# A reordered opening: batch 0's values loaded ahead of pairs 2 and 3, and the first MLP block begun with two pairs

## The chip, the cores and the metric

The kernel runs on one core of one Trainium2 chip. The metric is the device time of one execution in microseconds (us). Three runs of the kernel before gave 321.23, 321.58 and 321.67 us, a median of 321.58. Shorter is better.

## The reference

The input is q, k and v, each of 8 batches, 8 heads, 576 positions and 64 elements per head, and two matrices w_in (512 x 2048) and w_out (2048 x 512), all in float32. It is attention with a causal window of 64 keys, followed by a two-layer network with a hard-swish between:

```python
scores = scale * np.matmul(q, k.transpose(0, 1, 3, 2))
mask = (rel >= 0) & (rel < 64)            # rel = query position - key position
attn = softmax(np.where(mask, scores, -1e9))
x = np.matmul(attn, v)                    # to (8 * 576) tokens x 512
h = x @ w_in
g = h * np.clip(h + 3.0, 0.0, 6.0) / 6.0
out = g @ w_out                           # 4608 x 512
```

## The kernel before, in words

**Units of work.** The attention is done in pairs of heads: pair t is heads 2g and 2g + 1 of batch b, with t = 4b + g, so pairs 0 to 3 are batch 0 and pairs 4 to 7 are batch 1. The network is done in 9 blocks of 512 tokens (`kb`). Block 0 needs all four pairs of batch 0, since a token's 512 inputs are the outputs of 8 heads. For one block the *first product* gives 16 column blocks (`fc`), each the sum of four matmuls over groups g = 0 to 3, group g being the output of pair g (L485). ScalarE (ACT) and VectorE (DVE) then form hard-swish in `gT` (`hidden`, L497 and L498). The *second product* (L521) takes four token groups, each the sum over the 16 column blocks, and its results go out by L527 and L529.

**Batch 0** has a path of its own, the `_early` functions, once for each pair:

- `load_early_qk` (L108) loads a pair's queries and keys, two DMAs of 144 KB, and `load_early_v` (L127) all of the batch's values, four DMAs of 128 KB and one of 64 KB.
- `t_k` and `t_q` transpose them on TensorE (PE, L214) and copy them to `KT` (DVE, L232) and `QT` (ACT, L223). `t_q` also makes `QZ`, zero-padded copies of the last 64 queries, on DVE (L227).
- `s_early` forms the scores (L244 adds the mask by a product, L252 the scores, L257 those of the last keys from `QZ`), and ACT takes their exponentials (L259, L263).
- `shift_early` (L151, L153) makes a second arrangement of the values, shifted by 64 positions, chunk by chunk: chunk 0 on GpSimd (POOL), chunks 1 to 4 on DVE.
- `pv_early` (L352) multiplies weights with values, and DVE divides by the sums (L361, L362). Pairs 0 and 2 use a buffer of two banks, pairs 1 and 3 two separate banks.
- `x_early` transposes the result (L373), and ACT writes it to `xT` (L376), the input of the first product.

Batches from 1 on use `turn` (L274), `turned` (L281), `s_first`, `s_rest` (L308), `weights`, `pv` (L402), `pv_out` and `x_turned` or `x_`.

**What sets the order.** The schedule is written by hand: each engine runs its instructions in the order of the program text, and a wait holds up all that stands behind it on that engine. All loads go by POOL's one DMA queue, in the order in which POOL issues them, between POOL's other instructions. The order there is: pair 0, the identity's select (L669), pair 1, two selects for the mask (L190), pairs 2 and 3, the values, two parts of w_in of 512 KB (columns 0 to 511 and 512 to 1023, that is column blocks 0 to 3 and 4 to 7), POOL's two copies for chunk 0 (L151, L153), the third part of w_in of 1 MB, six selects for later masks (L197), the first half of w_out (L170), pairs 4 and 5 (L119), the second half of w_out, pairs 6 and 7, and batch 1's values (L138).

**PSUM.** There are eight banks: `ps_o` (one buffer of two banks), `ps_t` (three), `ps_h` (two) and `ps_acc` (one). A tile holds its bank until its last reader is done.

**PE's order in the opening.** 16 warm-up products on zeros (`warm`), transposes of pairs 0 and 1, scores of 0, transposes of 2, scores of 1, transposes of 3, scores of 2, scores of 3, four warm-up products, outputs of pairs 0 and 1, two warm-up products, `x_early(0)`, output of pair 2; then block 0's first product: group 0 of column blocks 0, 1 and 2, `x_early(1)`, output of pair 3, `x_early(2)`, group 1 of blocks 0 to 2, groups 0 and 1 of blocks 3 and 4 in the buffer of two banks (`pair_bank`), `x_early(3)`, group 2 of blocks 0 to 4, and group 3 of these (`complete`). Blocks 5 to 15 follow with all four groups at once. Then two units of the second product, the transposes of pair 4, two more units, and in a loop (L795 on) pairs 5 to 7 with units of the second product between them.

Of the kernel before, what the change touches and what calls it, by code (L numbers as in the profile page):

```python
# [10 lines left out]
F32 = mybir.dt.float32  # L11
# [3 lines left out]
MULT = mybir.AluOpType.mult  # L15
# [9 lines left out]
P = 128  # L25
D = 64
W = 64
# [9 lines left out]
def kernel(  # L37
# [61 lines left out]
    def load_early_qk(pairs, first=0):  # L99
        if first:  # L100
            tiles = staged[0]
        else:
            both = stage.tile([SP, 2, H, R * D], BF16, name="qk6", tag="qk")
            tiles = [both[:, 0], both[:, 1]]
        h = 2 * first
        for n in pairs:
            for t, src in zip(tiles, (q, k)):
                nc.gpsimd.dma_start(  # L108
                    out=t[:, h : h + 2 * n, :],
                    in_=src[0, h : h + 2 * n].rearrange("h (p r) d -> p h (r d)", r=R),  # L110
                )
# [12 lines left out]
    def load_early_v():  # L124
        for m in range(NM):
            n = min(P, S - m * P)
            nc.gpsimd.dma_start(  # L127
                out=Vn[0][:n, m, :, 0:D], in_=v[0, :, m * P : m * P + n, :].rearrange("h s d -> s h d"),
            )
# [28 lines left out]
        nc.sync.dma_start(out=us[0 : P - 32], in_=un[32:P])  # L158
        nc.sync.dma_start(out=us[P - 32 : P, 0], in_=un[0:32, 1])

    def load_w_in(i):
        n = FF // 4
        c = (slice(0, n), slice(n, 2 * n), slice(2 * n, FF))[i]
        nc.gpsimd.dma_start(
            out=win16[:, :, c], in_=moe_w_in[:, c].rearrange("(g p) f -> p g f", p=P)
        )

    def load_w_out(c):
        n = NFC // 2
        nc.gpsimd.dma_start(  # L170
            out=wout16[:, c * n : (c + 1) * n, :],
            in_=moe_w_out[c * n * P : (c + 1) * n * P, :].rearrange("(c p) j -> p c j", p=P),
        )
# [28 lines left out]
    def late_windows():  # L202

        for part in halves:
            select(band, part, -1, 1, -1, 0.0)
            select(band, part, W, -1, 1, 0.0)
            select(first, part, 0, -1, 1, 0.0)

    def transposed_heads(pool, src, g):

        tp = pool.tile([P, R, SP], BF16, name="tp", tag="bk")
        for r in range(R):
            for h in range(2):
                nc.tensor.transpose(  # L214
                    out=tp[h * D : (h + 1) * D, r, :],
                    in_=src[:, 2 * g + h, r * D : (r + 1) * D], identity=ident[:SP, :SP],
                )
        return tp

    def t_q(t):  # L220
        b, g = divmod(t, NG)
        tp = transposed_heads(ps_h, staged[b][0], g)
        nc.scalar.copy(  # L223
            out=QT[t][:].rearrange("q (p r) -> q p r", r=R), in_=tp[:].rearrange("q r p -> q p r"),
        )
        for h in range(2):
            nc.vector.tensor_copy(out=QZ[t][halves[h], h], in_=QT[t][halves[h], S - W : S])  # L227

    def t_k(t):
        b, g = divmod(t, NG)  # L230
        tp = transposed_heads(ps_acc, staged[b][1], g)
        nc.vector.tensor_copy(  # L232
            out=KT[t % 4][:, W:].rearrange("q (p r) -> q p r", r=R),
            in_=tp[:].rearrange("q r p -> q p r"),
        )
# [101 lines left out]
    def pv_early(t):  # L337
        b, g = divmod(t, NG)
        vn, vs, pz, pl = Vn[b % 2], Vs[b % 2], Pz[t % 4], Pl[t % 4]
        if t in (1, 3):  # L340
            os = [ps_h.tile([P, 1, 512], F32, name="oh", tag="bk") for _ in range(2)]
        else:
            os = [ps_o.tile([P, 2, 512], F32, name="o", tag="o")]
        n = len(os)
        for h in range(2):
            hh = 2 * g + h
            o = os[h % n][:, h // n]
            for m in range(NM):
                om = o[:, m * (D + 1) : (m + 1) * (D + 1)]
                for a in range(2):  # L350
                    last = m == NM - 1
                    nc.tensor.matmul(  # L352
                        om[a * W : (a + 1) * W], lhsT=pl[:, h, a * W : (a + 1) * W] if last else pz[:, h, m, a, :],
                        rhs=(vn if a and not last else vs)[:, m, hh, 0 : D + 1], start=True, stop=True,
                    )
        opg = work.tile([P, NM, 2, D], BF16, name="opg")
        for i, o in enumerate(os):
            hs = slice(i, i + 2 // n)
            ov = o[:, :, 0 : NM * (D + 1)].rearrange("p h (m c) -> p h m c", c=D + 1)
            rec = recs[:, t, hs, 0:NM]  # L360
            nc.vector.reciprocal(out=rec.unsqueeze(3), in_=ov[:, :, :, D : D + 1])  # L361
            nc.vector.tensor_tensor(  # L362
                out=opg[:, :, hs].rearrange("p m h d -> p h m d"), in0=ov[:, :, :, 0:D],
                in1=rec.unsqueeze(3).to_broadcast([P, 2 // n, NM, D]), op=MULT,
            )
        opgs[t] = opg

    def x_early(t):
# [98 lines left out]
    def first_units(kb):  # L467
        t0 = kb * TB % XR
        gT = gpool.tile([P, NFC, TB], BF16, name="gT")
        gTs[kb] = gT  # L470

        def unit(fc, gs=range(NG), pool=None, to=None, act=True):
            if fc in halfway:
                hT = halfway.pop(fc)
            elif to is not None:
                hT = to
            else:
                if pool is None:
                    if late[0] == 0:
                        pool = ps_acc if fc == 8 else ps_h if fc in (5, 6, 11, 12) else ps_t  # L480
                    else:
                        pool = ps_t if late[0] == 1 or fc % 2 else ps_h
                hT = pool.tile([P, TB], F32, name="hT", tag="bk")[:]
            for g in gs:
                nc.tensor.matmul(  # L485
                    hT, lhsT=win16[:, g, fc * P : (fc + 1) * P], rhs=xT[:, g, t0 : t0 + TB],
                    start=(g == 0), stop=(g == NG - 1),
                )
# [12 lines left out]

        units[kb] = unit, hidden
        return [lambda fc=fc: unit(fc) for fc in range(NFC)]

# [167 lines left out]
    )  # L672
    load_early_qk((1,), 1)
    window()
    load_early_qk((1,) * (NG - 2), 2)
    for t in KT:
        nc.vector.memset(t[:, 0:W], 0.0)
    for t in QZ:
# [3 lines left out]
    nc.vector.memset(first[:], 1.0)  # L682
    pads(1, nc.vector.memset)
    load_early_v()
    nc.vector.memset(Vs[0][0:W, 0], 0.0)
    for i in range(2):
        load_w_in(i)
    shift_early(0, nc.gpsimd.tensor_copy)
    load_w_in(2)
    late_windows()  # L690
    load_w_out(0)
    staged[1] = load_qk(1, 2)
    load_w_out(1)
    load_qk(1, 2, 2)
    load_v(1, True)
    nc.vector.memset(recs[:], 1.0)
    nc.vector.memset(Pl[0][:], 1.0)
    for t in Pl[1:]:
# [4 lines left out]

    warm(ps_h, 12)
    warm(ps_h, 4, W)
    t_k(0)
    t_q(0)
    t_k(1)
    t_q(1)
    s_early(0)  # L710
    t_k(2)
    t_q(2)
    s_early(1)
    t_k(3)
    t_q(3)
    s_early(2)
    for m in range(1, NM):
        shift_early(m, nc.vector.tensor_copy)
    s_early(3)
    warm(ps_acc, 4)  # L720
    pv_early(0)
    pv_early(1)
    warm(ps_acc, 2)
    x_early(0)
    pv_early(2)
    queue_block(0, 0)
    u = units[0][0]

    def inputs(gs, fcs, **to):
        for fc in fcs:  # L730
            u(fc, gs, **to)

    u(0, (0,), ps_acc)
    inputs((0,), (1, 2), pool=ps_t)
    x_early(1)
    pv_early(3)
    x_early(2)
    inputs((1,), range(3))
    for fc, to in zip((3, 4), pair_bank()):
        u(fc, (0, 1), to=to)  # L740
    x_early(3)
    inputs((2,), range(5))
    complete(0, range(5), (3, 4))
    def group(t, n):

        if t >= 2 * NG:
# [146 lines left out]
```

## Time and profile before

| what | value |
|---|---|
| median of three runs | 321.58 us |
| the profiled execution's own time | 321.83 us |
| its span in the trace | 320.0 us |
| PE busy | 302.5 us, 95% |
| DVE, ACT, POOL busy | 181.1, 184.3 and 124.1 us |
| PE busy from 4 to 14 us | 8.64 of 10 us |
| PE busy from 14 to 20 us | 4.87 of 6 us |
| PE busy from 20 to 40 us | 19.26 of 20 us |
| first product of block 0 begins (L485) | 20.30 us |
| last waiting-free stretch of that product | 26.50 to 36.00 us, 44 matmuls |
| granted clock of PE, mean | 0.996 |

The span is what the trace covers; 1.83 us of the execution's time lie outside it. Times in the trace are counted from the start of the span. "PE busy" counts the time in which at least one matmul was in the array, so that a busy PE isn't always at its peak rate; the products of 128x512 follow each other each 0.216 us in the stretch of 44. The first 40 us are read by the chain of waits, which says what each step was released by, by POOL's timeline, and by the DMA queue in windows.

### The profile page before, as it was taken

The page shows a single profiled execution, that of the slowest core. Times are in us where ns is not written, and L with a number is a line of the kernel's source. Part 1 is how long each engine was busy: PE and PEld are TensorE (multiplying, and loading weights), DVE is VectorE, ACT ScalarE, POOL GpSimd, SP SyncE. Part 2 cuts the span into 40 slices and gives each one's busy share as a digit, 9 for nine tenths or more (in the row PEclk, how much of TensorE's full clock was granted, in tenths as well). Part 3 has the DMA queues.
Part 4 walks back from the last instruction along what each step waited for, and adds up shares of the span by engine and source line. Part 5 has one row for each costly group of instructions (what it writes and reads, how often), then busy time and mean ns, then how long its engine had stood idle before and what let it go on. Part 6 is the DMA issues. An engine that isn't in the chain of part 4 may idle for free.

```text
span 320.0 us, 10694 instructions
## 1 busy us (share of the span) xinstructions
PE 302.5 (95%) x4566; PEld 152.2 (48%) x4608; DVE 181.1 (57%) x415; ACT 184.3 (58%) x345; POOL 124.1 (39%) x169
## 2 busy tenths in 40 slices
PE   7889998889999999999999999999999999999992
PEld 3454454444545555555555555555544444444440
DVE  5776747588747753775377627762776156334200
ACT  2737665578657764776477547764773366454310
POOL 8971204669785435553446335633330000000000
PEclk9999999999999999999999999999999999999998
DMA  7999995989999932994299339934021200100021
GB/s 93 164 203 207 207 189 116 173 146 111 179 124 167 131 116 88 167 128 117 88 155 140 108 98 154 144 102 103 5 63 43 84 33 0 69 33 34 36 74 66
DMA packets 57592, 35.67 MB, mean 111 GB/s; under 512 B 39872, under 2 KB 51648, under 8 KB 57536
## 3 DMA queue, kind: packets, MB, share of 16 engines
q0 software_dynamic: 35904, 18.81, 45.9%
q1 hardware_dynamic: 21632, 16.08, 20.6%
q8 instruction: 38, 0.62, 0.8%
q14 instruction: 18, 0.15, 0.1%
HBM read 37.62 MB, written 9.44 MB: 147 GB/s over the span
## 4 chain that ended last, share of the span: by engine, by line
PE 86%; DMA 5%; DVE 2%; issue 2%; ACT 2%; POOL 1%; SPq 0%; POOLq 0%; ACTq 0%
PE hT L485 37%; PE acc L521 35%; PE o L402 3%; PE s L308 3%; PE acco L521 2%; DMA V<-V 2%; PE tk L274 2%; DMA qk<-in_k_dram 2%; DMA xT<-opl 1%; POOL qk L108 1%; PE tq L274 1%; PE hTo L485 1%; DVE opl L426 0%; DVE V L151 0%; PE xp L373 0%
## 5 line engine op out<-in xcount | busy, mean ns | idle before, releaser
L498 DVE SCALAR_TENSOR_TENSOR gT<-t,hT 128x512 bf16<-128x512 bf16 x141 | 95.7, 686 | 77.7 <-ACT t L497 76.9
L485 PE MATMUL hT<-xT,win 128*128 128x512 bf16 x552 | 132.1, 379 | 0.9 <-ACT xT L376 0.3
L521 PE MATMUL acc<-wout,gT 128*128 128x512 bf16 x518 | 126.1, 379 | 2.4 <-issue 1.3
L497 ACT ACTIVATE t<-hT,half_const 128x512 bf16<-128x512 f32 x141 | 95.7, 689 | 50.0 <-PE hT L485 48.1
L485 PEld LDWEIGHTS <-win 128*128 128x128 bf16 x576 | 55.6, 98 | 66.2 <-issue 1.0
L521 PEld LDWEIGHTS <-gT 128*128 128x128 bf16 x576 | 54.3, 98 | 62.8
L329 POOL TENSOR_TENSOR Pz<-e,band 128x512 bf16<-128x512 bf16 x48 | 54.2, 1146 | 0.5 <-ACT e L321 0.4
L326 POOL TENSOR_TENSOR P<-e,first 64x256 bf16<-64x256 bf16 x24 | 15.9, 661 | 84.7 <-ACT e L317 84.6
L527 ACT COPY osb<-acc 128x512 f32<-128x512 f32 x34 | 19.9, 586 | 43.7 <-PE acc L521 43.7
L321 ACT ACTIVATE e<-s 128x512 bf16<-128x512 f32 x56 | 30.2, 593 | 0.9 <-PE s L308 0.7
L281 DVE COPY KT<-tk 128x576 bf16<-128x576 bf16 x28 | 21.0, 749 | 5.3 <-ACT e L317 4.5
L138 POOL DMA_DIRECT2D V<-in_v_dram x22 | 17.9, 819 | 11.6 <-DMA win<-in_moe_w_in_dram 5.2
L426 DVE TENSOR_TENSOR opl<-o,recs 128x256 bf16<-128x256 f32 x52 | 19.6, 419 | 0.5
L281 ACT COPY QT<-tq 128x576 bf16<-128x576 bf16 x28 | 17.8, 637 | 1.5 <-PE tq L274 1.5
L411 DVE TENSOR_REDUCE sums<-o 128x10 f32<-128x20 f32 x26 | 4.5, 175 | 24.3 <-PE o L402 24.3
L402 PEld LDWEIGHTS <-Pz 64*64 64x64 bf16 x1008 | 11.6, 108 | 13.3 <-issue 11.5
L308 PE MATMUL s<-QT,KT 64*64 64x64 bf16 x896 | 14.7, 195 | 0.5 <-issue 0.5
L317 ACT ACTIVATE e<-tk 64x128 bf16<-64x128 f32 x28 | 7.6, 270 | 12.5 <-PE tq L294 12.5
L402 PE MATMUL o<-V,Pz 64*64 64x65 bf16 x936 | 13.6, 195 | 1.2 <-DMA V<-V 1.2
L274 PE MATMUL tk<-ident,qk 64*64 64x64 bf16 x504 | 13.9, 195 | 0.3 <-DMA qk<-in_k_dram 0.3
L274 PE MATMUL tq<-ident,qk 64*64 64x64 bf16 x504 | 13.7, 195 | 0.4 <-DMA qk<-in_q_dram 0.4
L274 PEld LDWEIGHTS <-qk 64*64 64x64 bf16 x1008 | 11.5, 106 | 3.1 <-issue 1.7
(102 smaller groups left out, 196.6 us busy)
## 6 DMA issues: line engine op xcount, KB each, us to landing
out_dram<-osb SPq DMA_DIRECT2D x36, 256.0 KB, 2.3
V<-in_v_dram POOLq DMA_DIRECT2D x16, 256.0 KB, 5.7
V<-V SPq DMA_DIRECT2D x6, 432.0 KB, 4.3
qk<-in_k_dram POOLq DMA_DIRECT2D x4, 576.0 KB, 6.7
qk<-in_q_dram POOLq DMA_DIRECT2D x4, 576.0 KB, 9.7
wout<-in_moe_w_out_dram POOLq DMA_DIRECT2D x2, 1024.0 KB, 18.8
qk<-in_q_dram POOLq DMA_DIRECT2D x12, 144.0 KB, 4.3
qk<-in_k_dram POOLq DMA_DIRECT2D x12, 144.0 KB, 3.8
```

The costliest lines, as they stand in the source:

```text
L274: nc.tensor.transpose(out=hosts[t][z][halves[h], r * W : (r + 1) * W], in_=staged[b][halves[z], 2 * g + h, r * D : (r + 1) * D], identity= ...
L281: (nc.scalar.copy if z else nc.vector.tensor_copy)(out=(QT[t % 4][:] if z else KT[t % 4][:, W:]).rearrange("q (p r) -> q p r", r=RL), in_= ...
L308: nc.tensor.matmul(ss[h][halves[i], c, m, r], lhsT=keys(t, h, W * (w - 1), r), rhs=QT[t % 4][halves[h], w * W : (w + 1) * W], start=True, ...
L321: nc.scalar.activation(out=e[:].rearrange("p c m r w -> p (c m r w)"), in_=ss[h][:].rearrange("p c m r w -> p (c m r w)"), func=EXP, scale ...
L329: muls[h].tensor_tensor(out=Pw[t % 4][:, h].rearrange("p c m r w -> p (c m) (r w)"), in0=e[:].rearrange("p c m r w -> p (c m) (r w)"), in1 ...
L402: nc.tensor.matmul(o[i][halves[c], c0 : c0 + D + 1], lhsT=p, rhs=vt[:, hh, v0 : v0 + D + 1], start=(r == 0), stop=(r == 1), skip_group_che ...
L426: nc.vector.tensor_tensor(out=opg[:, :, i], in0=ov[i][:, 0:4, 1 : D + 1].rearrange("p (m h) d -> p m h d", h=2), in1=rec[:, i, 0:4].rearra ...
L485: nc.tensor.matmul(hT, lhsT=win16[:, g, fc * P : (fc + 1) * P], rhs=xT[:, g, t0 : t0 + TB], start=(g == 0), stop=(g == NG - 1),)
L497: nc.scalar.activation(out=t1[:], in_=hT, func=RELU, bias=half_const[:], scale=1.0 / 6.0)
L498: nc.vector.scalar_tensor_tensor(out=gT[:, fc, :], in0=t1[:], scalar=1.0, in1=hT, op0=MIN, op1=MULT)
L521: nc.tensor.matmul(acc, lhsT=gT[:, fc, ts * P : (ts + 1) * P], rhs=wout16[:, fc, :], start=(fc == 0), stop=(fc == NFC - 1),)
L527: nc.scalar.copy(out=osb[:], in_=acc)
```

## The change

- The loads of pairs 2 and 3 move behind the values. Pair 2's come right after them, then POOL's two shift copies, then pair 3's.
- The first part of w_in is loaded in two halves (groups 0 and 1, then 2 and 3), so there are four issues instead of three; all stand behind pair 3's.
- `QZ` is made by a function of its own, `padded`, on DVE for pairs 0 and 1 and on POOL for pairs 2 and 3. POOL's later issues (six selects, w_out, batch 1) come behind that of pair 3 in the program.
- PE's order: transposes of 0 and 1, scores of 0 and 1, four warm-up products, output of 0, transposes of 2, `x_early(0)`, output of 1, scores of 2, transposes of 3, `x_early(1)`, group 0 of column block 0, output of 2, scores of 3, group 0 of blocks 1 and 2, group 1 of blocks 0 to 2, `x_early(2)`, output of 3, groups 0 and 1 of blocks 3 and 4, group 2 of blocks 0 to 2, `x_early(3)`, group 2 of blocks 3 and 4, and group 3 of the five. Two warm-up products are left out.
- DVE's seven shift copies stand ahead of all of pairs 2 and 3's work.
- All pairs' outputs use the buffer of two banks, chunk by chunk with both heads in turn, with one reciprocal and one product on DVE. Column blocks 0 and 1 stand in `ps_h`, 2 in `ps_acc`, 3 and 4 in `ps_t`. Pair 3's transposes swap their pools.

```diff
-    def load_w_in(i):
+    def load_w_in(i, gs=slice(0, NG)):
...
-            out=win16[:, :, c], in_=moe_w_in[:, c].rearrange("(g p) f -> p g f", p=P)
+            out=win16[:, gs, c], in_=moe_w_in[gs.start * P : gs.stop * P, c].rearrange("(g p) f -> p g f", p=P)
...
-        for h in range(2):
-            nc.vector.tensor_copy(out=QZ[t][halves[h], h], in_=QT[t][halves[h], S - W : S])
+
+    def padded(t, move):
+        for h in range(2):
+            move(out=QZ[t][halves[h], h], in_=QT[t][halves[h], S - W : S])
...
-        if t in (1, 3):
-            os = [ps_h.tile([P, 1, 512], F32, name="oh", tag="bk") for _ in range(2)]
-        else:
-            os = [ps_o.tile([P, 2, 512], F32, name="o", tag="o")]
...
+        o = ps_o.tile([P, 2, 512], F32, name="o", tag="o")
+        for m in range(NM):
+            for h in range(2):
...
-                    if late[0] == 0:
-                        pool = ps_acc if fc == 8 else ps_h if fc in (5, 6, 11, 12) else ps_t
+                        pool = ps_acc if fc == 8 else ps_h if fc in (6, 7, 11, 12) else ps_t
...
     load_early_qk((1,), 1)
     window()
-    load_early_qk((1,) * (NG - 2), 2)
...
     load_early_v()
+    load_early_qk((1,), 2)
     nc.vector.memset(Vs[0][0:W, 0], 0.0)
-    for i in range(2):
-        load_w_in(i)
     shift_early(0, nc.gpsimd.tensor_copy)
-    load_w_in(2)
+    load_early_qk((1,), 3)
+    for gs, c in ((0, 0), (1, 0)):
+        load_w_in(c, slice(2 * gs, 2 * gs + 2))
+    for c in (1, 2):
+        load_w_in(c)
...
+    dve, pool = nc.vector.tensor_copy, nc.gpsimd.tensor_copy
+    for t in range(2):
+        t_k(t)
+        t_q(t)
+        padded(t, dve)
+    s_early(0)
+    s_early(1)
+    for m in range(1, NM):
+        shift_early(m, dve)
+    warm(ps_acc, 4)
+    pv_early(0)
+    t_k(2)
+    t_q(2)
+    padded(2, pool)
+    x_early(0)
+    pv_early(1)
+    s_early(2)
+    t_k(3)
+    t_q(3)
+    padded(3, pool)
     late_windows()
     load_w_out(0)
...
+    x_early(1)
     queue_block(0, 0)
...
+    inputs((0,), (0,), pool=ps_h)
+    pv_early(2)
+    s_early(3)
+    inputs((0,), (1,), pool=ps_h)
+    inputs((0,), (2,), pool=ps_acc)
+    inputs((1,), range(3))
+    x_early(2)
     pv_early(3)
-    x_early(2)
-    inputs((1,), range(3))
-    for fc, to in zip((3, 4), pair_bank()):
-        u(fc, (0, 1), to=to)
+    inputs((0, 1), (3, 4), pool=ps_t)
+    inputs((2,), range(3))
     x_early(3)
-    inputs((2,), range(5))
-    complete(0, range(5), (3, 4))
+    inputs((2,), (3, 4))
+    complete(0, range(5))
```

More of the change, by code (lines that the diff above doesn't have):

```diff
@@ L221, in t_q @@
         b, g = divmod(t, NG)
-        tp = transposed_heads(ps_h, staged[b][0], g)
+        tp = transposed_heads(ps_acc if t == NG - 1 else ps_h, staged[b][0], g)
         nc.scalar.copy(
@@ L225, in t_q @@
         )
+    def padded(t, move):
         for h in range(2):
-            nc.vector.tensor_copy(out=QZ[t][halves[h], h], in_=QT[t][halves[h], S - W : S])
+            move(out=QZ[t][halves[h], h], in_=QT[t][halves[h], S - W : S])
     def t_k(t):
         b, g = divmod(t, NG)
-        tp = transposed_heads(ps_acc, staged[b][1], g)
+        tp = transposed_heads(ps_h if t == NG - 1 else ps_acc, staged[b][1], g)
         nc.vector.tensor_copy(
@@ L339, in pv_early @@
         vn, vs, pz, pl = Vn[b % 2], Vs[b % 2], Pz[t % 4], Pl[t % 4]
-        if t in (1, 3):
-            os = [ps_h.tile([P, 1, 512], F32, name="oh", tag="bk") for _ in range(2)]
-        else:
-            os = [ps_o.tile([P, 2, 512], F32, name="o", tag="o")]
-        n = len(os)
-        for h in range(2):
[L346 to L349, printed above, removed]
+        o = ps_o.tile([P, 2, 512], F32, name="o", tag="o")
+        for m in range(NM):
+            for h in range(2):
+                om = o[:, h, m * (D + 1) : (m + 1) * (D + 1)]
                 for a in range(2):
@@ L353, in pv_early @@
                         om[a * W : (a + 1) * W], lhsT=pl[:, h, a * W : (a + 1) * W] if last else pz[:, h, m, a, :],
-                        rhs=(vn if a and not last else vs)[:, m, hh, 0 : D + 1], start=True, stop=True,
+                        rhs=(vn if a and not last else vs)[:, m, 2 * g + h, 0 : D + 1], start=True, stop=True,
                     )
         opg = work.tile([P, NM, 2, D], BF16, name="opg")
[L357 to L365, printed above, removed]
+        ov = o[:, :, 0 : NM * (D + 1)].rearrange("p h (m c) -> p h m c", c=D + 1)
+        rec = recs[:, t, :, 0:NM]
+        nc.vector.reciprocal(out=rec.unsqueeze(3), in_=ov[:, :, :, D : D + 1])
+        nc.vector.tensor_tensor(
+            out=opg[:].rearrange("p m h d -> p h m d"), in0=ov[:, :, :, 0:D],
+            in1=rec.unsqueeze(3).to_broadcast([P, 2, NM, D]), op=MULT,
+        )
         opgs[t] = opg
@@ L684 @@
     load_early_v()
+    load_early_qk((1,), 2)
     nc.vector.memset(Vs[0][0:W, 0], 0.0)
-    for i in range(2):
-        load_w_in(i)
     shift_early(0, nc.gpsimd.tensor_copy)
-    load_w_in(2)
[L690 to L695, printed above, removed]
+    load_early_qk((1,), 3)
[3 more added lines that the diff above has]
+        load_w_in(c)
     nc.vector.memset(recs[:], 1.0)
@@ L705 @@
     warm(ps_h, 4, W)
[L706 to L709, printed above, removed]
-    s_early(0)
+    dve, pool = nc.vector.tensor_copy, nc.gpsimd.tensor_copy
[3 more added lines that the diff above has]
+        padded(t, dve)
+    s_early(0)
+    s_early(1)
[3 more added lines that the diff above has]
+    pv_early(0)
     t_k(2)
     t_q(2)
-    s_early(1)
+    padded(2, pool)
+    x_early(0)
+    pv_early(1)
+    s_early(2)
     t_k(3)
     t_q(3)
[L716 to L725, printed above, removed]
+    padded(3, pool)
+    late_windows()
+    load_w_out(0)
+    staged[1] = load_qk(1, 2)
+    load_w_out(1)
+    load_qk(1, 2, 2)
+    load_v(1, True)
+    x_early(1)
     queue_block(0, 0)
@@ L731, in inputs @@
             u(fc, gs, **to)
-    u(0, (0,), ps_acc)
-    inputs((0,), (1, 2), pool=ps_t)
-    x_early(1)
+    inputs((0,), (0,), pool=ps_h)
[5 more added lines that the diff above has]
+    x_early(2)
     pv_early(3)
-    x_early(2)
-    inputs((1,), range(3))
-    for fc, to in zip((3, 4), pair_bank()):
-        u(fc, (0, 1), to=to)
+    inputs((0, 1), (3, 4), pool=ps_t)
+    inputs((2,), range(3))
     x_early(3)
-    inputs((2,), range(5))
-    complete(0, range(5), (3, 4))
+    inputs((2,), (3, 4))
+    complete(0, range(5))
     def group(t, n):
```

## The prediction

> **What bounds the kernel now.** I read the page first: its totals and its chain that ended last.
>
> ```profile
> PE 302.5 (95%) x4566; PEld 152.2 (48%) x4608; DVE 181.1 (57%) x415; ACT 184.3 (58%) x345; POOL 124.1 (39%) x169
> PE 86%; DMA 5%; DVE 2%; issue 2%; ACT 2%; POOL 1%; SPq 0%; POOLq 0%; ACTq 0%
> ```
>
> PE (TensorE) is busy for 302.5 of 320.0 us. The change leaves its work alone but for two warm-up products fewer (0.22 us each), so it can only move idle time, and it touches only what stands before 36 us. I asked for the chain of the first 50 us next.
>
> ```profile
> 5.60 5.06 DMA qk<-in_k_dram
> ...
> 26.50 9.50 PE hT L485 x44
> ...
> 42.53 1.73 PE acc L521 x8
> 44.26 0.14 PE tk L274
> ```
>
> The chain waits for pair 2's keys until 10.66, goes through small steps on PE, ACT and DVE, and from 26.50 it is products without a gap. At 44.26 stands the first transpose of pair 6 (batch 1's third pair), with no wait ahead. Its data come by GpSimd's (POOL's) DMA queue; the issues of that queue, with the time to landing, show when:
>
> ```profile
> qk<-in_k_dram POOLq DMA_DIRECT2D x1, 288.0 KB, 22.3
> qk<-in_q_dram POOLq DMA_DIRECT2D x1, 288.0 KB, 23.1
> ```
>
> The queries of pairs 6 and 7 were issued at 20.91 and land 23.1 later, at 44.0. PE comes for them at 44.2. **So some 0.2 us behind PE runs the load stream**: whatever the opening saves is given back here unless the stream is earlier too. That stream is what I reckon with. POOL's timeline issues it in this order:
>
> ```profile
> 5.60 0.63 POOL L108 DMA_DIRECT2D qk<-in_k_dram  x1
> 6.22 0.63 POOL L108 DMA_DIRECT2D qk<-in_q_dram  x1
> 6.84 0.63 POOL L108 DMA_DIRECT2D qk<-in_k_dram  x1
> 7.46 4.22 POOL L127 DMA_DIRECT2D V<-in_v_dram  x5
> 11.62 1.55 POOL L164 DMA_DIRECT2D win<-in_moe_w_in_dram  x2
> 13.22 0.66 POOL L151 COPY V<-V 64x576 bf16<-64x576 bf16 x1
> 13.94 0.66 POOL L153 COPY V<-V 64x576 bf16<-64x576 bf16 x1
> 14.55 0.74 POOL L164 DMA_DIRECT2D win<-in_moe_w_in_dram  x1
> ```
>
> The two copies (batch 0's shifted values, first chunk) now stand behind 1 MB of w_in already issued, so they cost the stream nothing: the stretch table has it at 158 GB/s from 4 to 14 us, 188 to 20 us, 208 from 20 to 40, without a break.
>
> **The change, part by part.**
>
> *The stream.* The software queue in half-microsecond windows has moved 0.59 MB (pairs 0 and 1) by about 7.15 us, 1.18 MB by 10.7, 1.77 MB (all of batch 0) by 14.5. So the values take 3.9 us, and a pair's 0.295 MB takes 1.75 us once supplied. From an issue to its first packet I take 1.4 us: the first issue, at 1.38, has packets from 2.8, and an issue into an idle queue at 50.96 has them between 52.1 and 52.35. After the change POOL goes on at 4.96 with the values, to 4.96 + 4.22 = 9.18; pair 2 (two issues of 0.63), to 10.45; then the two copies, which took 13.17 to 14.55, 1.4 us, to 11.85. Their data, the first chunk, then landed at most 1.5 us after its bytes moved (7.15 + 0.85), at 9.5, so they need not wait. Only then come pair 3's issues. Moved: values 7.15 to 11.05, pair 2 to 12.8, **pair 3 not before 11.85 + 1.4 = 13.25**, to 15.0. The queue is empty for 0.45 us, and w_in starts at 15.0 instead of 14.5: 0.5 us late. Everything behind w_in in the queue (w_out, batch 1) is late by as much, since from there the queue is always full.
>
> Ends: without a gap 11.05 + 3.5 = 14.55, no loss, and with pair 2 at the fastest half-microsecond row (0.09 MB) 14.35, 0.15 us early. On the other side the copies can be held up by DVE, which now makes its own seven shift copies at the same time: of two DVE copies of QZ in POOL's copy window one took 565 ns instead of 178. Two such hold-ups the other way round, 0.39 us each, make 0.5 + 0.8 = 1.3 late. I take 0.6, nearest to the plain sum, with part of one hold-up.
>
> That copies of the two engines exclude each other is also what the Trainium skill says (SBUF — State Buffer, "Who interferes with whom"): GpSimd and a VectorE copy in a two-port mode share one port pair, and the second fully blocks. The 565 ns row agrees; that a DVE copy also stops POOL's DMA issues, as the page has it, this trace does not show (issues of 0.63 to 0.67 us under DVE's memsets at 2 to 4 us).
>
> *The queue's later issues.* w_out and batch 1 now stand behind the QZ copies of pairs 2 and 3 on POOL, and the latter wait for ACT's copy of pair 3, at about 18.5 us; with two copies and the six selects (2.0 us, 15.35 to 17.28) w_out is issued at some 21 instead of 17.28. The queue still has w_in to move until 25, so this is covered by 2.5 us. If that cover were gone, each us would count in full. One issue more for w_in (0.75 us on POOL at 14) lies under transfers. Each DMA waits for the eighth before it (POOL's waits at 22.73 on w_in show that); none of those is later than its successor's turn.
>
> *The opening on PE.* QZ by POOL instead of DVE: bounded by a 1x1 copy (0.18) and a 64x576 one (0.66), I take 0.2 each; pair 2's stand behind w_in's issues, until 16.5. That holds the last product of pair 2's scores, at a time when pair 3 (landing 16.5) is not there either. Pairs 1 and 3 now use one reciprocal and product (0.22 + 0.82) in place of two of each (2 x 0.18 + 2 x 0.49): 0.3 us less DVE each, and the same 20 matmuls. Values are in at 11.05 + 1.5, the last shift copy at about 13, so pair 0's output product moves from 17.07 to some 13, and block 0's first product with pair 0 from 20.30 to some 18, when w_in's first half is in. All this gains nothing by itself: column block 4 needs the second part of w_in, which lands at 22.5 (12.4 + 10.1) now and at 23.1 then. Behind it stand, in order, two products of block 4 (0.43), three of group 2 (0.65), pair 3's transposes (0.29), ACT's copy of them (0.73 with its gaps) and five closing products (1.08): 3.2 us, so 26.3 where it is 26.50 now. **The opening gains 0.2 us at w_in's pace** (0.8 less the delay), not the 2 to 4 us by which its first steps move. From there the 44 products run as before: banks of blocks 0 and 1 come free at 0.69 us per block of DVE against 0.865 on PE.
>
> *What is late next.* PE would reach pair 6 at 44.06; its queries land at 44.0 + 0.6, plus 0.1 for the semaphore: 44.7. So **PE waits 0.65 us, and is 0.45 us behind the old 44.26**. Pairs 4 and 5 (35.9 + 0.6 against 37.66), w_out's second half (41.1 + 0.6 against 42.53) and batch 1's values (49.2 + 0.6 against 50.23) hold nothing. Between 44.26 and 49.9 the chain is all PE, and what follows is released by it, so the 0.45 us stays to the end.
>
> Sum: span 320.0 + 0.45; the profiled execution's 321.83 becomes 322.28. The median of the runs shown is 0.25 below that execution, so I forecast **322.0**.
>
> **Rivals.**
>
> *No gap* (0.13): the queue holds out during the copies. The stream is then 0 to 0.15 early, pair 6 is met 0 to 0.3 us sooner: 321.3 to 321.6. For it: the margin is 0.45 us of estimates. Against: the windows from 5.8 to 6.4 us, just 1.4 us behind POOL's selects, fall to 106 GB/s from 171, so pauses of POOL are seen in the queue.
>
> *POOL held up* (0.24): DVE's seven copies block POOL's, or pair 2 moves faster and the gap is 1 us and more: w_in 1.1 to 1.9 late, which passes through pair 6 less 0.15: 322.5 to 323.3.
>
> *The stream is early and the opening counts* (0.22): w_in's start and the rate after it give pairs 6 and 7 before 43.4. The PE side then decides: 0.8 at 26.5, up to 1.3 with w_in half a us early: 320.3 to 320.9. It is worth over 0.64 us only if the landing moves from 44.0 to 43.4 or sooner. For it: from 40 to 46 the DMA moves only 183 GB/s, so a stream that is less disturbed there could gain that. Against: up to 14.5 the same bytes move with one pause more.
>
> *A new wait on PE* is in the forecast: pair 6. That the change does nothing at all would be the no-gap case.
>
> **Chances.** 0.2% of this time is 0.64 us, about what a measurement of this kernel tells from no change. The forecast case (0.41) runs from 321.7 to 322.5, and 322.22 cuts it: 0.25 within, 0.16 slower. No gap 0.13 within; POOL held up 0.24 slower; early stream 0.22 faster. So 0.22 faster, 0.38 within, 0.40 slower. The range reaches to 320.7 and 323.1, which leaves out half of the early case and the end of the held-up one.
>
> **What would show it.** On POOL's timeline the two copies between pair 2's and pair 3's issues at 10.4 to 11.9, pair 3's first issue at 11.8 to 12.6; the DMA share falling near 12.8 to 13.3; the w_in parts landing some 0.5 us later; the first L485 product near 18 us; PE waiting on w_in ahead of block 4, then on DMA qk at L274 near 44.7 for 0.4 to 0.8 us; after that all stages shifted alike. I would be wrong if pairs 6 and 7 land before 43.4, if PE isn't waiting there at all, or if a later stage shows a difference of its own.

## The result, and the profile after

The changed kernel is slower: a median of 323.84 us over 22 runs (321.91 to 326.12) beside 321.37 us over 22 runs of the kernel before, a ratio of 1.0078 with a 95% interval of 1.0056 to 1.0101. The forecast was 322.0 us, within 320.7 to 323.1. The profiled execution took 324.99 us, with a span of 323.2: above the median of the 22, so the profile shows 3.2 us of loss where the medians show 2.5.

The page's totals and its chain that ended last, of the kernel after:

```profile
PE 303.0 (94%) x4563; PEld 152.3 (47%) x4606; DVE 180.3 (56%) x407; ACT 184.3 (57%) x345; POOL 125.8 (39%) x174
PE 82%; DMA 4%; DVE 4%; POOL 3%; ACT 2%; issue 2%; SPq 0%; POOLq 0%; ACTq 0%; DVEq 0%
```

PE's busy time is nearly the same (303.0 against 302.5 us); its share of the chain fell, since the span grew around it. The chain of the first 46 us says where (start, length, what):

```profile
13.08 7.46 DMA win<-in_moe_w_in_dram
20.54 0.58 issue
21.13 0.76 PE o L348 x20
21.89 0.97 PE sc L246 x2
...
28.29 8.14 PE hT L479 x37
...
39.02 1.73 PE acc L515 x8
```

The waits for w_in, of PE and of its weight loads (PEld):

```profile
PE o L348 <- DMA win<-in_moe_w_in_dram: 2.9, 1, 2.9
PEld L479 <- DMA win<-in_moe_w_in_dram: 2.5, 1, 2.5
```

The chain comes down POOL's issues to the first half of w_in, issued at 13.08 and in at 20.54. The 0.58 us called "issue" behind it hold the first product itself: its weights (L479) load from 20.59 to 20.70, and its own row is missing from the trace. Then pair 2's output (L348) and pair 3's scores (L246) follow, though neither reads w_in, and the five closing products begin at 28.29, where they began at 25.42 before. The second product begins at 39.02, where it began at 36.00: all 3 us of the profile's loss are made before 39 us. From there the two kernels run alike; pair 6's transposes stand at 47.28 instead of 44.26.

The stretch table of the changed kernel, one microsecond a line (PE busy comes second; the last three columns are the granted clock, the DMA share and GB/s), and two lines of the kernel before:

```profile
15.00:16.00 1.00, 1.00 (x41) 0.83 (x35) 0.76 (x1) 0.63 (x2) 1.00 (x2) 1.00 0.59 75
16.00:17.00 1.00, 1.00 (x29) 0.48 (x24) 0.77 (x2) 0.55 (x2) 0.51 (x3) 1.00 0.60 63
17.00:18.00 1.00, 1.00 (x33) 0.83 (x31) 0.61 (x2) 0.94 (x2) 0.00 (x0) 1.00 0.66 84
18.00:19.00 1.00, 0.26 (x5) 0.09 (x2) 0.42 (x1) 1.00 (x4) 0.09 (x1) 1.00 0.96 153
19.00:20.00 1.00, 0.00 (x0) 0.00 (x0) 0.00 (x0) 0.39 (x1) 0.82 (x4) 1.00 1.13 181
20.00:21.00 1.00, 0.00 (x0) 0.11 (x1) 0.00 (x0) 0.00 (x0) 0.86 (x4) 0.74 1.24 206
21.00:22.00 1.00, 0.87 (x21) 0.76 (x22) 0.07 (x1) 0.00 (x0) 1.00 (x3) 0.50 1.24 213
22.00:23.00 1.00, 1.00 (x12) 0.22 (x11) 0.97 (x2) 0.00 (x0) 1.00 (x3) 0.50 1.25 211
23.00:24.00 1.00, 1.00 (x20) 0.65 (x15) 0.01 (x1) 0.57 (x2) 1.00 (x2) 0.55 1.15 210
```

```profile
15.00:16.00 1.00, 0.89 (x19) 0.30 (x17) 0.94 (x3) 0.46 (x2) 0.87 (x4) 1.00 1.27 180
...
17.00:18.00 1.00, 0.82 (x36) 0.66 (x37) 0.50 (x3) 0.34 (x2) 1.00 (x3) 1.00 1.23 195
```

Three things are to be seen. From 15 to 18 us the queue moves 63 to 84 GB/s, though POOL has issued all of w_in by 16.0; before, the same stretch had 180 to 195. PE is idle from 18.3 to 20.6, some 2.3 us; the 2.9 us that the row of waits gives, and that some expectations below take over, count in the first product, whose row is missing. And from about 20.5 to 23.9 the granted clock is 0.50, just when PE has work again.

### The profile page after: what moved, and what is told of

Read it like the earlier page. It is cut to its first block, busy times and chain, and to the rows that moved or that the text cites. A ratio compares the mean times of both kernels' runs of the same rounds, so it can differ in the third digit from the quotient of the medians.

```text
span 323.2 us, 10686 instructions
## 1 busy us (share of the span) xinstructions
PE 303.0 (94%) x4563; PEld 152.3 (47%) x4606; DVE 180.3 (56%) x407; ACT 184.3 (57%) x345; POOL 125.8 (39%) x174
## 4 chain that ended last, share of the span: by engine, by line
PE 82%; DMA 4%; DVE 4%; POOL 3%; ACT 2%; issue 2%; SPq 1%; POOLq 0%; ACTq 0%; DVEq 0%
PE hT L479 36%; PE acc L515 34%; PE o L396 3%; DMA win<-in_moe_w_in_dram 2%; PE s L310 2%; PE acco L515 2%; PE tk L276 2%; POOL qk L108 2%; DMA xT<-opg 1%; POOL V L127 1%; DVE gT L492 1%; ACT t L491 1%; DVE opl L420 1%; PE tq L276 1%; DVE KT L283 1%
## 5 line engine op out<-in xcount | busy, mean ns | idle before, releaser
L492 DVE SCALAR_TENSOR_TENSOR gT<-t,hT 128x512 bf16<-128x512 bf16 x143 | 97.2, 687 | 78.0 <-ACT t L491 77.4
L479 PE MATMUL hT<-xT,win 128*128 128x512 bf16 x559 | 134.1, 379 | 2.7 <-DVE gT L492 1.0
L491 ACT ACTIVATE t<-hT,half_const 128x512 bf16<-128x512 f32 x143 | 97.2, 690 | 51.9 <-PE hT L479 50.3
L479 PEld LDWEIGHTS <-win 128*128 128x128 bf16 x576 | 55.8, 98 | 71.1 <-issue 4.0
L521 ACT COPY osb<-acc 128x512 f32<-128x512 f32 x34 | 19.9, 587 | 43.7 <-PE acc L515 43.7
```

The costliest lines, as they stand in the source:

```text
L479: nc.tensor.matmul(hT, lhsT=win16[:, g, fc * P : (fc + 1) * P], rhs=xT[:, g, t0 : t0 + TB], start=(g == 0), stop=(g == NG - 1),)
L492: nc.vector.scalar_tensor_tensor(out=gT[:, fc, :], in0=t1[:], scalar=1.0, in1=hT, op0=MIN, op1=MULT)
L521: nc.scalar.copy(out=osb[:], in_=acc)
```

## The experiments

Each kernel is the changed one, or the one before, with the edits shown; the ratio is to runs of the kernel before on the same chip. "Closing" is the start of the five closing products in the profiled execution (25.42 before, 28.29 after).

| kernel | ratio, 95% interval | closing, us |
|---|---|---|
| changed | 1.0078, 1.0056 to 1.0101 | 28.29 |
| scores first | 1.0028, 1.0003 to 1.0052 | 26.44 |
| shift copies on DVE | 1.0012, 0.9978 to 1.0046 | 25.91 |
| filler in the wait | 1.0042, 1.0014 to 1.0070 | 26.89 |
| w_in's first part whole | 1.0117, 1.0064 to 1.0170 | 28.71 |
| first half of w_in into the pause | 1.0015, 0.9992 to 1.0039 | 26.29 |
| both mends | 1.0019, 0.9995 to 1.0042 | 25.37 |
| both mends and early w_in | 1.0020, 0.9992 to 1.0047 | 28.00 |
| loads alone | 1.0138, 1.0116 to 1.0159 | 31.75 |
| order alone | 1.0124, 1.0105 to 1.0142 | 29.73 |
| old kernel with the pause | 1.0047, 1.0018 to 1.0076 | 25.41 |

Two more kernels (without DVE's shift copies, w_out first) were run once each, for the load stream alone, and have no ratio.

### Scores first

```diff
-    inputs((0,), (0,), pool=ps_h)
     pv_early(2)
     s_early(3)
+    inputs((0,), (0,), pool=ps_h)
     inputs((0,), (1,), pool=ps_h)
```

> The changed kernel with one move on PE: the first product of column block 0 with pair 0 goes behind pair 2's output and pair 3's scores. Theory A, the order on PE: that product waits for the first half of w_in until 20.5 us, and work that needs no w_in stands behind it; then this kernel does pair 2's output near 18.5 and pair 3's scores near 19, is through the five closing products some 1.7 us sooner (bounded by the second part of w_in, landing at 24.5, and 3.2 us behind it), and the granted clock stays at full; the ratio to the kernel before is 1.000 to 1.004. Theory B, the load stream that is late by 1.3 us at pair 6: nothing is gained, since what PE saves it waits for later; ratio 1.006 to 1.010. Pair 6's landing near 45.3 us allows up to 1.9 us.

The ratio fell to 1.0028, as theory A had it; theory B, the one on record, allowed no gain and falls as the main cause. The chain of waits in this kernel, from the closing products on:

```profile
26.44 10.73 PE hT L479 x49
```

The closing products come 1.85 us sooner than in the changed kernel. w_in's first half, issued at 13.16, landed at 19.5, and PE had other work until 21.6, so its lateness cost nothing here. One part of the expectation failed: the clock did fall in this profile, at another place, to 0.50 from 9.3 to 16 us, after PE had waited 1.8 us for pair 1. So this profile is not at its best either.

### Shift copies on DVE

```diff
-    shift_early(0, nc.gpsimd.tensor_copy)
...
-    for m in range(1, NM):
+    for m in range(NM):
         shift_early(m, dve)
```

> The changed kernel with POOL's two shift copies of the values' first chunk made by DVE, ahead of its other seven, so that POOL issues pair 3 right behind pair 2. If the pause on POOL makes w_in late, the first half of w_in is issued at 11.7 instead of 13.1 and lands at 19.0 to 19.3 instead of 20.5, pair 6 lands 0.4 to 1.3 us sooner than 45.3, and the kernel gains 1.3 us, or up to 2.3 us if PE's idle time gets so short that the granted clock doesn't fall: ratio 1.000 to 1.004. If the stream is bound by its bytes and not by the pause, w_in lands at 20 or later and the ratio stays at 1.006 to 1.010.

Without POOL's pause the first half of w_in is issued at 11.67 and lands 6.5 us later, at 18.2, and PE no longer waits for it; the ratio is 1.0012. So the loss needs the pause: taking it away, with PE's order unchanged, takes most of the loss away. This profile too has a halved clock, from 9.2 to 16.0 us, behind a wait of 1.4 us for pair 1.

### Filler in the wait

```diff
+    warm(ps_acc, 8)
     inputs((0,), (0,), pool=ps_h)
```

> The changed kernel with eight warm-up products on zeros (1.7 us) put on PE ahead of the first product of column block 0, in the time in which PE waits for w_in. Theory C, the clock: the granted clock of 0.50 from 20.5 to 23.9 us is the consequence of 2.9 us of idle PE, and stretches the work of these 3.4 us by some 1.0 us; with the filler the clock stays at full and the kernel gains 0.8 to 1.0 us, ratio 1.004 to 1.006. If the clock costs nothing that the loads don't hide, or falls anyway, the ratio stays at 1.007 to 1.010.

The ratio is 1.0042, at the end of the expected range, but its interval overlaps that of the changed kernel, so the medians only point to it. The profile says more. PE's timeline in this kernel:

```profile
18.84 1.89 PE L657 MATMUL wt<-zeros 128*128 128x512 bf16 x8 [0.64 <-ACT QT L223]
20.57 0.38 PE L479 MATMUL hT<-xT,win 128*128 128x512 bf16 x1
```

The half of w_in landed at 19.5 in this execution (13.23 + 6.3), under the filler, so part of the profile's gain is its earlier landing. The first product starts at 20.57, the moment at which its weights load in the changed kernel (20.59). From there to the closing products it is 6.3 us here, at a full clock, and 7.7 us there, 3.4 of them at half: by this comparison of two executions the clock cost some 1.4 us. I had estimated 1.0.

### w_in's first part whole

```diff
-    for gs, c in ((0, 0), (1, 0)):
-        load_w_in(c, slice(2 * gs, 2 * gs + 2))
-    for c in (1, 2):
+    for c in range(3):
         load_w_in(c)
```

> The changed kernel with the first part of w_in loaded whole again, three issues instead of four. If the half's slow arrival (7.5 us from issue to landing, while the 512 KB part took 7.7 us in the kernel before) is a cost that each first transfer of w_in has whatever its size, the whole part lands at 20.6 to 20.9, the second part up to 0.75 us sooner, and the ratio is unchanged within 0.2%, 1.006 to 1.010. If halving has brought the first product forward, the whole part lands later than 21.3, and the ratio rises to 1.010 or more. If halving itself slows the stream, w_in lands before 20 and the ratio falls below 1.005.

The whole part landed at 20.76, 7.7 us after its issue, hardly later than the half did. That doesn't separate size from slow start, since in this execution the queue was back at 155 GB/s from 17 to 18 us, where the changed kernel had 84. The ratio of 1.0117 is above the expected range, but with an interval that holds most of it. Whether halving gains anything stays open.

### First half of w_in into the pause

```diff
     load_early_qk((1,), 2)
+    load_w_in(0, slice(0, 2))
     shift_early(0, nc.gpsimd.tensor_copy)
     load_early_qk((1,), 3)
-    for gs, c in ((0, 0), (1, 0)):
-        load_w_in(c, slice(2 * gs, 2 * gs + 2))
+    load_w_in(0, slice(2, 4))
```

> The changed kernel with one load moved: the first half of w_in's first part is issued right behind pair 2, ahead of POOL's two shift copies and pair 3, so that the queue has 256 KB to move during POOL's pause. PE's order is unchanged. If the loss comes of that half landing late (20.5 us in the profile of the changed kernel, with PE waiting 2.9 us and the clock at 0.50 after it), it now lands at 16 to 18, PE waits less than 0.5 us for it, no interval of halved clock follows, and the ratio to the kernel before falls from 1.008 to 1.000 to 1.003. Pair 3 lands up to 1.3 us later, which is the price; if that is what counts, or if PE's order itself costs the time, the ratio stays at 1.005 or more.

The half, issued at 10.37, lands 6.0 us later, at 16.4, and the ratio is 1.0015. PE's order is the changed one, the pause is there, and most of the loss is gone: what counts is when that half lands. The longest waits of PE from 6 to 30 us are now for pairs 1 and 2, and w_in is not among PE's waits:

```profile
PE tp L214 <- DMA qk<-in_k_dram: 2.5, 2, 1.2
```

The part on the clock failed: this profile shows 0.5 from 16.2 to 19.6, after waits of 1.2 us each for pairs 1 and 2.

### Both mends

The first product behind pair 3's scores, and all shift copies on DVE.

```diff
-    shift_early(0, nc.gpsimd.tensor_copy)
...
-    inputs((0,), (0,), pool=ps_h)
     pv_early(2)
     s_early(3)
+    inputs((0,), (0,), pool=ps_h)
...
-    for m in range(1, NM):
+    for m in range(NM):
```

> Both mends together: pair 2's output and pair 3's scores ahead of the first product (ratio 1.0028 alone), and the first chunk's shift copies on DVE (1.0012 alone). If both mend the same wait for w_in, the two do no better than the better one: 1.000 to 1.003. If each takes away a cost of its own, their gains of 0.50% and 0.66% add up and the kernel is faster than the one before: 0.996 to 0.998.

1.0019: no better than either alone, which fits that both mend the same wait. In this profile the clock stayed full, and the closing products begin at 25.37, just where they do in the kernel before. Yet the span is 320.7 us, 0.7 longer than before. The chain of waits says where a part of it comes from:

```profile
25.86 18.84 DMA qk<-in_q_dram
...
44.73 0.21 PE tq L276
```

PE is at pair 6 and waits 0.22 us for its queries, which land at 44.7 instead of 44.0. (It stops once more, for 0.56 us ahead of pair 7's transposes at 48.27; what released that stop, the trace doesn't show.) This is the wait that the prediction named, at the time that it gave (44.7), and it comes to light only once the bigger one is gone. But the reason that the prediction gave for it, POOL's pause ahead of pair 3, isn't in this kernel, so that the time agrees is luck; why the stream is late here stays open.

### Both mends and early w_in

Against the kernel with both mends:

```diff
+    load_w_in(0, slice(0, 2))
     load_early_qk((1,), 3)
-    for gs, c in ((0, 0), (1, 0)):
-        load_w_in(c, slice(2 * gs, 2 * gs + 2))
+    load_w_in(0, slice(2, 4))
```

> Both mends of the earlier run (first product behind pair 3's scores, all shift copies on DVE) and, besides, the first half of w_in's first part issued ahead of pair 3, so that the w_in stream is begun while the queue still has 1.3 us and more of other data. If what is left of the loss (1.0019 with both mends, where PE waits at pair 6 for queries landing at 44.7 us instead of 44.0) is the slow start of w_in in the queue, pair 6 lands at 44.0 to 44.4 and the ratio is 0.998 to 1.001. If pair 3, which now comes later, is what counts, the ratio is 1.002 to 1.005.

1.0020 with an interval that holds 1: undecided. Pair 6 landed at 45.3, not at 44.0 to 44.4, and pair 3 at 19.1, for which PE waited 2.1 us, with a halved clock behind it. Starting w_in sooner thus didn't bring the stream forward; the version that beats the kernel before wasn't found.

### Loads alone, and order alone

The kernel before with the new order of loads, and the changed kernel with the old one (first diff against the kernel before, second against the changed one).

```diff
-    load_early_qk((1,) * (NG - 2), 2)
...
+    load_early_qk((1,), 2)
-    for i in range(2):
-        load_w_in(i)
     shift_early(0, nc.gpsimd.tensor_copy)
-    load_w_in(2)
+    load_early_qk((1,), 3)
+    for gs, c in ((0, 0), (1, 0)):
+        load_w_in(c, slice(2 * gs, 2 * gs + 2))
+    for c in (1, 2):
+        load_w_in(c)
```

```diff
+    load_early_qk((1,) * (NG - 2), 2)
...
-    load_early_qk((1,), 2)
+    for i in range(2):
+        load_w_in(i)
     shift_early(0, nc.gpsimd.tensor_copy)
-    load_early_qk((1,), 3)
-    for gs, c in ((0, 0), (1, 0)):
-        load_w_in(c, slice(2 * gs, 2 * gs + 2))
-    for c in (1, 2):
-        load_w_in(c)
+    load_w_in(2)
```

> The kernel before with the new order of loads alone (values ahead of pairs 2 and 3, w_in's first part in halves, POOL's copies between pairs 2 and 3); PE's order is the old one, with all four pairs' scores ahead of the first output. Pair 3 lands near 16.7 us instead of 12.2, so pair 3's scores end near 19.5 instead of 16.2, and the outputs behind them come 2 to 3 us later: ratio 1.006 to 1.009. If the old order on PE hides the later pair 3 (it has work to do with the values, which come sooner), the ratio is 1.001 to 1.004, and the loss of the full change belongs to its PE order.

> The changed kernel with the old order of loads (pairs 0 to 3, values, w_in in three parts with POOL's copies ahead of the third): PE's new order alone. Pair 0's output now stands ahead of pair 2's transposes and needs the values, whose last shift copy ends near 17 us; so pairs 2 and 3 are behind by 5 us and more though their data are there at 12.2, and w_in, at 19.3, is waited for by nobody: ratio 1.005 to 1.009 if PE's order is bound by the values, 1.000 to 1.003 if the stretch behind (one pair's steps beside another's) makes up for it.

Both are worse than the whole change, 1.0138 and 1.0124, and above what I expected. The longest waits of PE in the opening, first for the loads alone, then for the order alone:

```profile
PE tp L214 <- DMA qk<-in_k_dram: 5.0, 2, 4.0
```

```profile
PE o L348 <- DVE V L151: 2.2, 4, 0.7
PE o L348 <- POOL V L151: 1.2, 1, 1.2
```

With the old order PE comes for pair 2's keys 4.0 us early; with the old loads the values' shifted copies are late. Both profiles show the clock halved behind these gaps (0.50 from 13 to 23, and from 17 to 23). The two parts of the change need each other: each alone costs more than both together.

### Without DVE's shift copies

The seven copies are left out; chunks 1 to 4 of the shifted values stand as ones.

```diff
-    nc.vector.memset(Vs[0][0:W, 0], 0.0)
+    nc.vector.memset(Vs[0][:], 1.0)
...
-    for m in range(1, NM):
-        shift_early(m, dve)
```

> The changed kernel without DVE's seven shift copies; the shifted values of chunks 1 to 4 are left out and stand as ones, so that this run is for the w_in stream alone. If the slow start of w_in (60 to 90 GB/s from 15 to 17.5 us, after POOL has issued all of it by 16.0) comes of DVE's copies holding up POOL's making of transfers, it is gone: above 150 GB/s from 15 us on, and the first half lands before 18.5. If it belongs to the transfers themselves, the dip stays and the half lands at 19.5 to 20.5 as in the other runs.

The slow start is still there, and the half lands at 20.3 (one execution, 325.0 us):

```profile
15.00:16.00 1.00, 1.00 (x27) 0.62 (x24) 0.67 (x2) 1.00 (x2) 1.00 (x2) 1.00 0.75 95
16.00:17.00 1.00, 1.00 (x26) 0.54 (x26) 0.82 (x1) 0.49 (x2) 0.51 (x3) 1.00 0.59 65
17.00:18.00 1.00, 0.95 (x29) 0.71 (x25) 0.65 (x1) 1.00 (x4) 0.00 (x0) 1.00 0.72 74
```

So these seven copies don't make it. This was the rule of the Trainium skill that I had weighed in the prediction (SBUF — State Buffer, "Who interferes with whom", by which a VectorE copy can keep GpSimd from making its transfers); for these copies it is not what happens here. DVE's other work, 0.65 to 0.82 us in each of these three, stayed and wasn't tested, and the rows that the prediction held against the rule were of memsets, not of copies.

### w_out first

The first half of w_out ahead of w_in, right behind pair 3.

```diff
+    load_w_out(0)
     for gs, c in ((0, 0), (1, 0)):
...
     late_windows()
-    load_w_out(0)
```

> The changed kernel with the first half of w_out (1 MB, whole rows) issued ahead of w_in, right behind pair 3: for the stream alone, since w_in lands 5 us later and PE waits for it. If the slow start is w_in's own (its pattern of 2 KB pieces out of rows of 8 KB), w_out starts at full rate: no dip below 150 GB/s from 15 to 18 us. If it is what any transfer does that is issued less than 2.5 us before the queue runs out of older data, the same dip to 60 to 90 GB/s stands at 15 to 17.5 us with w_out's packets.

The same dip, with w_out ahead in the queue (one execution, 330.4 us, in which PE waits for the later w_in):

```profile
15.00:16.00 1.00, 0.97 (x26) 0.79 (x27) 0.68 (x2) 1.00 (x2) 1.00 (x2) 1.00 0.75 106
16.00:17.00 1.00, 0.96 (x19) 0.40 (x18) 0.96 (x2) 0.33 (x2) 0.96 (x3) 1.00 0.74 78
17.00:18.00 1.00, 0.46 (x15) 0.31 (x16) 0.04 (x1) 1.00 (x3) 0.45 (x2) 1.00 0.94 119
```

So it isn't w_in's own pattern of access: w_out at this place starts slowly too.

### The old kernel with the pause

```diff
-    for i in range(2):
-        load_w_in(i)
     shift_early(0, nc.gpsimd.tensor_copy)
-    load_w_in(2)
+    for i in range(3):
+        load_w_in(i)
```

> The kernel before with one move: POOL's two shift copies stand ahead of all of w_in's issues, so that the old order of loads (pairs 0 to 3, values, w_in) gets the pause of 1.4 us, with w_in issued at 13.1 instead of 11.6 while the values still move until 14.5. If a short lead alone makes the slow start (w_in issued 1.4 us before the queue runs out, instead of 2.9), the rate dips below 120 GB/s between 14.5 and 17.5 us, w_in's first part lands 1.0 to 2.0 us later than 19.3, and the ratio is 1.002 to 1.006. If the slow start needs more than that (to follow on loads of 96 partitions, or an empty queue), the rate stays above 150 GB/s, w_in lands at 19.0 to 19.8, and the ratio is 0.998 to 1.002.

POOL's copies waited 1.3 us for their values (landing at 13.0), so w_in was issued at 14.37, later than expected. The stretch table:

```profile
15.00:16.00 1.00, 0.89 (x20) 0.45 (x20) 0.94 (x3) 0.37 (x3) 1.00 (x3) 1.00 0.64 24
16.00:17.00 1.00, 0.95 (x9) 0.34 (x10) 0.91 (x3) 1.00 (x3) 0.93 (x2) 1.00 0.61 55
17.00:18.00 1.00, 0.68 (x36) 0.60 (x38) 0.50 (x3) 0.20 (x2) 0.88 (x3) 1.00 1.21 202
```

The queue runs dry at 15 and is at full rate by 17. w_in's first part lands at 19.9, only 0.6 us late, and PE hardly notices. But the stream behind is late, and the ratio is 1.0047. The chain of the opening is now one line, and POOL:

```profile
22.19 22.79 DMA qk<-in_q_dram
...
45.02 0.21 PE tq L274
```

Pair 6's queries land at 45.0 instead of 44.0, and PE waits 0.63 us for them and begins at 45.02 instead of 44.26. Here the prediction's mechanism stands alone: a pause on POOL ahead of w_in, a gap in the queue, and 0.8 us lost at pair 6, of the 1.5 us by which this span is longer (321.5).

## Why the prediction was wrong, point by point

**POOL's timeline and the pause** were right. The copies ran from 10.50 to 11.88 (10.45 to 11.85 on record), pair 3's issues began at 11.84, w_in's at 13.08. POOL's lines of the changed kernel:

```profile
10.50 0.66 POOL L151 COPY V<-V 64x576 bf16<-64x576 bf16 x1
11.22 0.66 POOL L153 COPY V<-V 64x576 bf16<-64x576 bf16 x1
11.84 0.64 POOL L108 DMA_DIRECT2D qk<-in_q_dram  x1
...
13.08 2.96 POOL L164 DMA_DIRECT2D win<-in_moe_w_in_dram  x4
```

Pair 3 landed at 16.8 (16.5 on record). w_out was issued at 21.29 (some 21), and the queue was full by then, as the sum had it.

**The failed step is "block 0's first product with pair 0 from 20.30 to some 18, when w_in's first half is in".** The prediction shows no row of w_in for the 18; it follows from the start at 15.0 and the full rate from there. The rows have 63 to 84 GB/s for three microseconds, and the half lands at 20.54. The queue had moved 2.03 MB (batch 0's 1.77 and the half's 0.26) only by 18.75; at the 180 to 195 GB/s of before, from 15.0, it would have been 16.4, and with the 1.5 us that the prediction takes from bytes to landing some 18. So the pace of the queue was the wrong term; the landing 1.8 us behind the bytes is near what it took. The same slow start made the delay of the stream, 0.6 in the sum, 1.9 us at block 4's part of w_in (24.4 instead of 22.5) and 1.3 at pair 6. A row of before could have warned: w_in's first part took 7.7 us from issue to landing there too, under cover of the values ahead of it in the queue.

**What was queued behind that product was not counted.** The prediction listed what stands behind block 4, whose part of w_in it put at 23.1 (24.4 by the run). It did not list what stands behind the very first product: pair 2's output, pair 3's scores and all that hangs on them, 6.3 us of PE work from the first product to the closing ones. At 20.5 these end at 26.9 at full clock, later than block 4's condition would have asked in the forecast (26.3 less the closing products' 1.1) and a little later than it asks by the run's own landing (24.4 and 3.2 less 1.1, some 26.5). So of the 2.9 us by which the closing products are late, an estimate from these rows gives 1.1 to block 4's late weights, 0.4 to what is queued behind the first product, and 1.4 to the clock. Moving the product behind that work, or landing its half at 16.4, takes most of the loss away, with intervals that lie below that of the changed kernel. That both do so shows the cause: the late landing, paid by PE's order.

**The clock was left out.** PE idle for 2.3 us was followed by 3.4 us at 0.50, which cost some 1.4 us of that execution. The Trainium skill (TensorE: Matmul & The Clock Gate, "What's actually happening") gives half the clock for a window of about 3.4 us after an idle one, and windows that run free of the kernel. The trace agrees on the half and the length: with 0.74 from 20 to 21, 0.50 to 23 and 0.55 to 24 it is 3.4 us at half. It doesn't show an idle window of that length: PE was idle for 2.3 us here, and for 1.2 us at most at a time ahead of the halved stretch with w_in in the pause. That the windows fall where they may also fits the runs' spread (321.91 to 326.12 us; the ten runs with a mean granted clock up to 0.991 have a median of 324.5, the other twelve 323.5) and the halved stretches at other places in other profiles; that it causes the spread was not tested.

**Pair 6** was named as the wait that decides. In the changed kernel it decides nothing: its queries land at 45.3 (24.93 + 20.4), 1.3 us late where 0.6 was forecast, and PE comes at 47.28. With both mends and in the old kernel with the pause PE does wait there, 0.22 and 0.63 us. In the old kernel with the pause the whole mechanism is seen; with both mends only the place and the time, without the pause. So this mechanism exists, but second in line.

**"POOL held up"**, the rival nearest to the outcome, was priced up to 323.3 but by way of pair 6; that is not the way in which the time was lost. DVE's copies were held up beside POOL's (0.70, 0.69 and 0.49 us, 0.30 alone), but POOL's took 0.66, as before (0.82 and 0.78 for one copy in two other runs, the filler and w_in in the pause).

**Open:** why the queue starts so slowly behind pair 3. Six runs narrow it. Not DVE's shift copies, and not w_in's pattern or its halves (69 and 73 GB/s from 15 to 17 us with the whole part). Behind the values with a short lead (the old kernel with the pause) the queue runs dry and is back at full rate 2.6 us after the issue. Behind pair 3 without the pause it dips at 15 to 16 us, to 131 GB/s (shift copies on DVE) and 108 (both mends); behind pair 3 with the pause it creeps until 18 in the changed kernel and is at full rate only at 20, 7 us after the issue. So the pause and what stands ahead both play a part, and which property of pair 3's loads matters was not tried.

## What to carry to other kernels

Before a product is moved up, list what stands behind it on its engine that doesn't need what it waits for: that work pays the whole wait if the load is late. Take a load's landing from the row of the same kind of load, with what covered it there, not from a mean rate; and a pause on the issuing engine ahead of a big load can cost even where nobody waits for that load, because what stands behind it in the queue moves too (in the old kernel with the pause, w_in by 0.6 us and pair 6's queries by 1.0). An idle stretch of PE can cost more than its length: 2.3 us of it here brought some 1.4 us more for the clock.

## What the runs showed of the hardware

- A load of 256 KB landed 6.0 to 7.5 us after its issue behind pairs' loads (16.4 from 10.37; 20.5 from 13.08), and one of 512 KB in 5.5 us behind the values, from 14.37 with the queue running empty. I had expected size and backlog to set it.
- Three executions of nearly the same opening show the halved clock at three places (9.3 to 16, 16.2 to 19.6, 20.5 to 23.9 us), each behind a wait of PE of 1.2 to 2.3 us. A wait doesn't always bring it: with both mends PE waited 1.8 and 1.7 us, with the filler 2.2 us (for pair 1), and the clock stayed at 1.00 from 8 to 25 us.
